# One 96-row product for the sink columns of both heads, written beside the second head's transposes

## The chip, the cores and the metric

The kernel runs on one core of a Trainium2 chip. The metric is the time of one execution on the device in microseconds (us). The core's engines are called TensorE (PE in rows; PEld is its weight load), VectorE (DVE), ScalarE (ACT), GpSimd (POOL) and SyncE (SP, which only issues transfers here).

## The reference

Attention with a sliding window and a few sink positions, then a feed-forward layer with a gate:

```python
scores = scale * q @ k^T                      # 4 batches, 8 heads, 768 positions, head size 64
keep = is_sink | ((rel >= 0) & (rel < window))   # n_sink = 4, window = 128
a = softmax(where(keep, scores, -1e9))
x = (a @ v)  -> (3072, 512)                   # heads side by side
h = x @ w_in                                  # 512 -> 2048
out = (h * clip(h + 3, 0, 6) / 6) @ w_out     # 2048 -> 512
```

## The kernel before

**Tiling.** The positions of a batch fall into three *units* of 256 queries. A unit has four *pairs* of heads (two heads of 64 rows fill 128 partitions), so there are 12 units and 48 pairs. In the first unit of a batch the sinks lie in the window's own tiles; in the other two units they don't, and the first 16 positions (SK) are handled apart. This concerns 32 of the 48 pairs, and these alone are changed. Attention of one pair is interleaved with the feed-forward layer of an earlier unit, whose products fill TensorE.

**Precision.** Most products are made of three terms, high*high, low*high and high*low: each operand is split into a rounded high part and the remainder. `high` is made by a copy (ScalarE or VectorE), `low` by a subtraction on VectorE.

**Order.** The first 14 pairs follow a list that a planner writes (`in_order`). From then on a loop over steps `s` runs eight stages (`STAGES`, L827), each a string of short names, and after each stage one piece of the feed-forward layer is issued (`drain(1)`: 12 products `hps` of 256 columns, or 6 products `o` of 512). The engines execute in just this order. In step s the pair s-1 is scored, normalised and transposed (`C`, `t0`, `t1`, `X`, `c`, `N`, `S`, `D0`, `D1`), and the pair s-2 is multiplied with the values (`E0`, `E1`) and put together (`a0`, `a1`, `b0`, `b1`, `x`). `F` runs what the feed-forward layer owes on ScalarE and VectorE (`gf`, `gh`, `g`). The pool `ps` for TensorE's results has eight banks under one tag (`bank`), handed out as they come free.

**The sinks before.** `S` (C_sinks) takes the probabilities of the 16 sink columns of both heads and both query tiles out of `Pt` and splits them into `ssc` (per tile 64 columns: high of both heads, low of both heads). `D1` (D_pt of head 1) transposes head 1's probabilities into the bank `pt`, and between these transposes TensorE turns `ssc` around by a product with the identity into a bank of its own, `spt` (64 rows x 256). At the start of the next step ScalarE copies that to `pz` (`z`, D_sinks). In `E0` and in `E1` each head then multiplies `pz` with its own 128 columns of `vs` (the sink values, high and low) as the last of the seven products that add up in `av`:

```python
seq += [low[0], (sinks["v"][:, p, vsl], d["pz"], acc)]      # L637, once per head
```

`a0`, `a1` (E_low, ScalarE) move one half of `av` to `tmp`, `b0`, `b1` (E_sum, VectorE) add the other half, and `x` (E_split, VectorE) splits `tmp` into `xh` and `xl`, the feed-forward layer's input.

Of the kernel before, what the change touches and what calls it, by code (L numbers as in the profile page):

```python
# [10 lines left out]
F32 = mybir.dt.float32  # L11
F32R = mybir.dt.float32r
# [192 lines left out]
def attn_ffn_kernel(ctx: ExitStack, tc: tile.TileContext, qx, kx, vx, vfx, vsx, n_sink, window, w_in, w_out, out):  # L205
# [87 lines left out]
    def weng(which, at):  # L293
        return {"D": nc.vector, "P": nc.gpsimd, "A": nc.scalar}[which[at % len(which)]]
# [52 lines left out]

    ssc = work.tile([P, 2, 4 * SK], F32R, name="ssc", bufs=1)
    pz = work.tile([P, UT], F32R, name="pz", bufs=1)
# [14 lines left out]
    def batch_loads(b):  # L364
        if not sinks:
            sinks["v"] = work.tile([P, NP, 4 * D], F32R, tag="vs", name="vs", bufs=1)
            nc.gpsimd.memset(sinks["v"].bitcast(F32), 0.0)
        v4 = sinks["v"][0:4 * SK].rearrange("p a (h d) -> p a h d", h=4)
        raw_s = work.tile([P, NP, 2, D], F32, tag="st", name="raw_s", bufs=3)[0:4 * SK]
        nc.sync.dma_start(out=raw_s, in_=vsx[b])  # L370
        sinks["to"] = (v4, raw_s)

    def batch_split():
        v4, raw_s = sinks["to"]
        split_parts(nc, v4[:, :, 0::2, :], v4[:, :, 1::2, :], raw_s, nc.scalar, nc.vector)

    SSE = "DD"
    START = 9
    GHI, GLO = "AD", "DD"
    XHI, XLO = "DDA", "DD"  # L380

# [160 lines left out]
    def C_sinks(s):  # L542
        u = pus[s][1]
        d = st_[s]
        if u:

            ss = ssc.rearrange("p t (k h y) -> p t k h y", k=2, h=2)
            snk_in = d["P"].rearrange("p h t w -> p h (t w)")[:, :, 2 * P:2 * WP].rearrange(
                "p h (t y) -> p t h y", t=2)[:, :, :, 0:SK]
            split_parts(nc, ss[:, :, 0], ss[:, :, 1], snk_in, weng(SSE, 0), weng(SSE, 1))  # L550

    def D_pt(s, h):
        b, u, p = pus[s]
        d = st_[s]
        blocks = ((0, P), (1, 0)) if u else ((0, 0), (1, 0), (1, P))
        pt = ps.tile([P, 512], F32, tag="bank", name="pt")
        if u and h == 1:
            d["spt"] = ps.tile([P, 512], F32, tag="bank", name="spt")
        for j, (t, c) in enumerate(blocks):
            nc.tensor.transpose(out=pt[:, j * P:(j + 1) * P], in_=cell(s, h, t, c, c + P), identity=ident)  # L560
            if u and h == 1:
                nc.tensor.matmul(out=d["spt"][0:4 * SK, t * P:(t + 1) * P], lhsT=ssc[:, t, :], rhs=ident_r,
                                 start=True, stop=True)
        d[f"pt{h}"] = pt
# [36 lines left out]
    def D_sinks(s):  # L601
        u = pus[s][1]
        d = st_[s]
        if u:
            nc.scalar.copy(out=pz[0:4 * SK], in_=d["spt"][0:4 * SK, 0:UT])
            d["pz"] = pz

    def E_av(s, h):
# [13 lines left out]
        if plain(s):  # L622
            pf = d[f"pt{h}"]
            seq = [(VS[:, slot, h, :], pf[:, c:c + o1 - o0], d["av"][:, 0, o0:o1]) for slot, c, o0, o1 in ops]
        else:

            ph, pl = d[f"pt{h}"]
            vsl = slice(2 * D * h, 2 * D * (h + 1))
            vhi = slice(2 * D * h, 2 * D * h + D)
            high = [(VS[:, slot, vsl], ph[:, c:c + o1 - o0], acc[:, o0:o1]) for slot, c, o0, o1 in ops]  # L630
            low = [(VS[:, slot, vhi], pl[:, c:c + o1 - o0], acc[0:D, o0:o1]) for slot, c, o0, o1 in ops]
            seq = [high[0]]
            for a, l in zip(high[1:], low[1:]):
                seq += [a, l]

            if u:
                seq += [low[0], (sinks["v"][:, p, vsl], d["pz"], acc)]  # L637
            else:
                seq.append((VS[:, 0, vsl], pl[:, 0:UT], acc))
        for j, (l, r, o) in enumerate(seq):  # L640
            nc.tensor.matmul(out=o, lhsT=l, rhs=r, start=(j == 0 and (h == 0 or not plain(s))),  # L641
                             stop=(j == len(seq) - 1 and (h == 1 or not plain(s))))
        if h == 1:
            E_x(s)

# [22 lines left out]
    def E_sum(s, h):  # L668
        d = st_[s]
        rows = d["tmp"][ROWS[h]]  # L670
        nc.vector.tensor_tensor(out=rows, in0=d["av"][ROWS[h], h, :], in1=rows, op=ALU.add)

    def E_split(s):
# [127 lines left out]
    def do(name, e):  # L801
# [18 lines left out]
        else:  # L820
# [5 lines left out]

    STAGES = ("b F z", "C F t0 V1", "E0 E1 t1 m F Kh Qh", "F a0 a1 X Kl Ql b0 b1", "c V2 F N", "S F x v", "D0 F vs p0 o0",  # L827
              "D1 F p1 o1 L")

    def stage(s, steps):  # L830
# [10 lines left out]
                  "b0": lambda: E_sum(e, 0), "a1": lambda: E_low(e, 1), "b1": lambda: E_sum(e, 1),  # L841
                  "x": lambda: E_split(e)}
        for step in steps.split():
# [143 lines left out]
def _layout(q, k, v, n_sink, window, moe_w_in, moe_w_out):  # L987
# [25 lines left out]
    for h in range(2):  # L1013
        vfx[:, :, :, :, h, h] = vp[:, :, 0:2 * T, h].reshape(B, NP, 2, T, D).transpose(0, 1, 3, 2, 4)
    vsx = _np.zeros((B, 4, 16, NP, 2, D), v.dtype)
    for r in range(4):
        vsx[:, r, :, :, r % 2] = vp[:, :, 0:16, r % 2].transpose(0, 2, 1, 3)
# [4 lines left out]
            'vfx': vfx.reshape(B, NP, T, 2, 2, 2 * D),  # L1022
            'vsx': vsx.reshape(B, 64, NP, 2, D), 'n_sink': n_sink, 'window': window, 'w_in': w_in, 'w_out': w_out}

# [25 lines left out]
```

## Time and profile before

| | |
|---|---|
| median of 3 runs | 712.82 us (712.49 to 713.53) |
| profiled execution, its own time | 712.8 us |
| its span, first to last instruction | 711.0 us |
| TensorE busy / weight loads busy | 700.6 us (99%) / 623.6 us (88%) |
| VectorE busy / ScalarE busy | 505.4 us (71%) / 447.7 us (63%) |
| mean granted clock of TensorE | 0.999 of full speed |

The span is what the rows below cover; 1.8 us of the execution lie outside it. Products on TensorE overlap in the records (each is entered with its whole passage through the array), so the step from one start to the next is what a product costs, not its duration.

### The profile page before, as it was taken

Reading aid. Unit: us, or ns where it says so; the run is one execution under the profiler, and the core shown is the slowest. Engines: PE = TensorE matmul, PEld = TensorE weight load, DVE = VectorE, ACT = ScalarE, POOL = GpSimd, SP = SyncE. Lnnn points to the kernel's source line nnn. Section 1 sums busy time; section 2 is a strip of 40 time slices with the busy share of each in tenths; the row PEclk is TensorE's granted clock in tenths of the full one; section 3 lists DMA queues with packets and bytes.
Section 4 is the critical chain, followed back from the end, with each engine's and each line's share of the span. In section 5 each row is a group of like instructions: output and inputs, shape, how many; then the busy total and the mean of one; then the engine's idle time right before and its main releaser. Section 6 shows DMA issues by size and latency. Waiting matters only on the chain.

```text
span 711.0 us, 13205 instructions
## 1 busy us (share of the span) xinstructions
PE 700.6 (99%) x4940; PEld 623.6 (88%) x4940; DVE 505.4 (71%) x1327; ACT 447.7 (63%) x1171; POOL 4.9 (1%) x18
## 2 busy tenths in 40 slices
PE   8999999999999999999999999999999999999996
PEld 7888988898989898889988898889898989899995
DVE  5999997445677777777777777777777877775221
ACT  5999876655675666566656566566656665754222
POOL 2000000000000000000000000000000000000000
PEclk9999999999999999999999999999999999999999
DMA  7675662120111111211111012101111111100000
GB/s 250 195 217 186 194 207 72 61 67 27 39 62 60 31 49 43 68 31 61 31 61 60 31 39 89 32 31 61 60 40 31 61 58 35 60 12 0 31 1 35
DMA packets 29481, 49.45 MB, mean 70 GB/s; under 512 B 3552, under 2 KB 20448, under 8 KB 29408
## 3 DMA queue, kind: packets, MB, share of 16 engines
q1 hardware_dynamic: 29120, 48.51, 21.3%
q8 instruction: 41, 0.67, 0.4%
q14 instruction: 32, 0.26, 0.1%
q10 hardware_dynamic: 288, 0.00, 0.0%
HBM read 42.21 MB, written 6.29 MB: 68 GB/s over the span
## 4 chain that ended last, share of the span: by engine, by line
PE 82%; ACT 7%; DVE 6%; DMA 3%; issue 1%; ACTq 0%; DVEq 0%; SPq 0%
PE o L724 34%; PE hps L692 33%; PE av L641 7%; PE sp L497 5%; PE pt L560 3%; ACT Ph L524 2%; DMA st<-in_w_out_dram 1%; DVE st L338 1%; DVE wt L341 1%; ACT wt L333 1%; ACT st L335 1%; ACT Ph L538 1%; DMA raw<-in_window_dram 1%; DVE wil L346 1%; DMA st<-in_w_in_dram 1%
## 5 line engine op out<-in xcount | busy, mean ns | idle before, releaser
L692 PE MATMUL hps<-xh,wih 128*128 128x256 f32 x768 | 221.9, 289 | 0.0
L692 PE MATMUL hps<-xl,wih 128*128 128x256 f32 x768 | 216.6, 282 | 0.0
L692 PE MATMUL hps<-xh,wil 128*128 128x256 f32 x768 | 216.2, 282 | 0.0
L724 PE MATMUL o<-woh,gh 128*128 128x512 f32 x384 | 155.7, 406 | 0.2 <-ACT gh L195 0.2
L724 PE MATMUL o<-woh,g 128*128 128x512 f32 x384 | 151.6, 395 | 0.7 <-DVE g L710 0.7
L724 PE MATMUL o<-wol,gh 128*128 128x512 f32 x384 | 151.0, 393 | 0.0
L692 PEld LDWEIGHTS hps<-xh,wih 128*128 128x128 f32 x768 | 144.7, 188 | 2.1 <-issue 0.7
L692 PEld LDWEIGHTS hps<-xl,wih 128*128 128x128 f32 x768 | 144.8, 189 | 1.2
L692 PEld LDWEIGHTS hps<-xh,wil 128*128 128x128 f32 x768 | 144.7, 188 | 0.0
L195 ACT ACTIVATE ph<-pm 128x512 fp32r<-128x512 f32 x64 | 40.5, 632 | 108.5 <-DVE pm L572 108.5
L704 DVE SCALAR_TENSOR_TENSOR gf<-gf,hps 128x512 f32<-128x512 f32 x96 | 65.7, 684 | 47.4 <-ACT gf L701 47.2
L701 ACT ACTIVATE gf<-hps,three 128x512 f32<-128x512 f32 x96 | 65.4, 681 | 51.3 <-PE hps L692 51.2
L710 DVE TENSOR_TENSOR g<-gf,gh 128x512 fp32r<-128x512 f32 x96 | 66.4, 691 | 40.0 <-ACT gh L195 37.8
L724 PEld LDWEIGHTS o<-woh,g 128*128 128x128 f32 x384 | 72.1, 188 | 18.1 <-DVE g L710 1.5
L724 PEld LDWEIGHTS o<-woh,gh 128*128 128x128 f32 x384 | 72.3, 188 | 16.6 <-issue 3.1
L724 PEld LDWEIGHTS o<-wol,gh 128*128 128x128 f32 x384 | 72.5, 189 | 11.0
L598 DVE TENSOR_TENSOR pl<-pm,ph 128x512 fp32r<-128x512 f32 x64 | 44.3, 693 | 44.7 <-ACT ph L195 44.7
L195 ACT ACTIVATE gh<-gf 128x512 fp32r<-128x512 f32 x91 | 56.9, 625 | 26.7 <-DVE gf L704 25.9
L524 ACT ACTIVATE Pt<-Pt,nb 128x144 f32<-128x144 f32 (+2 forms) x144 | 58.8, 410 | 1.2
L666 ACT COPY tmp<-av 64x256 f32<-64x256 f32 x72 | 26.5, 368 | 35.4 <-PE av L641 34.8
L507 DVE CUSTOM_DVE_ANT_0 Pt<-sp,m_t 128x272 f32<-128x272 f32 x128 | 48.5, 435 | 0.0
L538 ACT ACTIVATE Pt<-Pt,rc 128x144 f32<-128x144 f32 (+2 forms) x142 | 47.5, 408 | 0.0
(100 smaller groups left out, 966.5 us busy)
## 6 DMA issues: line engine op xcount, KB each, us to landing
st<-in_w_in_dram SPq DMA_DIRECT2D x16, 512.0 KB, 4.7
st<-in_w_out_dram SPq DMA_DIRECT2D x16, 512.0 KB, 4.4
kr<-in_kx_dram SPq DMA_DIRECT2D x32, 200.0 KB, 2.6
qr<-in_qx_dram SPq DMA_DIRECT2D x48, 128.0 KB, 2.8
out_dram<-ost SPq DMA_DIRECT2D x24, 256.0 KB, 2.2
vr<-in_vx_dram SPq DMA_DIRECT2D x32, 192.0 KB, 2.4
VF<-in_vfx_dram SPq DMA_DIRECT2D x12, 256.0 KB, 4.0
kr<-in_kx_dram SPq DMA_DIRECT2D x16, 128.0 KB, 3.4
```

The lines of the kernel that those rows point to most:

```text
L195: nc.scalar.mul(out=out, in_=src, mul=scale)
L497: nc.tensor.matmul(out=sp[g][:, 0:w], lhsT=l[gs], rhs=r[gs], start=(j == 0), stop=(j == len(terms) - 1))
L507: nc.vector.tensor_tensor_reduce(out=cell(s, g, t, 0, w), in0=sp[g][:, 0:w], in1=m[:, 0:w], scale=-SCALE, scalar=3.0e38, op0=ALU.add, op1= ...
L524: nc.scalar.activation(out=blk, in_=blk, func=AF.Exp, scale=-1.0, bias=d["nb"][:, i:i + 1], accum_out=d["sm"][:, i:i + 1])
L538: nc.scalar.mul(out=blk, in_=blk, mul=c)
L598: nc.vector.tensor_tensor(out=pl[:, 0:w], in0=pt[:, 0:w], in1=ph[:, 0:w].bitcast(F32), op=ALU.subtract)
L641: nc.tensor.matmul(out=o, lhsT=l, rhs=r, start=(j == 0 and (h == 0 or not plain(s))), stop=(j == len(seq) - 1 and (h == 1 or not plain(s))))
L692: nc.tensor.matmul(out=hp[:, half, :], lhsT=l, rhs=r, start=(j == 0), stop=(j == n - 1))
L701: nc.scalar.activation(out=gf, in_=hp, func=AF.Relu, bias=three, scale=1.0)
L704: nc.vector.scalar_tensor_tensor(out=gf, in0=gf, scalar=6.0, in1=hp, op0=ALU.min, op1=ALU.mult)
L710: nc.vector.tensor_tensor(out=g, in0=gf, in1=gh.bitcast(F32), op=ALU.subtract)
L724: nc.tensor.matmul(out=acc, lhsT=l[:, f, ts_], rhs=r[i][:, f, :], start=(i == 0 and f == 0 and j == 0), stop=(i == NFP - 1 and f == 1 and ...
```

## The change

The sinks leave the two heads' sums. `ssc` gets 96 columns per tile: high of both heads, the same high again, low of both heads; ScalarE makes the second copy of the high part. `vs` gets 128 columns per head pair in place of 256: its rows are ordered so that one product over 96 rows gives high*high, high*low and low*high of both heads at once, head 0 in rows 0 to 63 of the result and head 1 in rows 64 to 127. TensorE turns `ssc` around into the right half of `pt`'s bank of head 1, and the new product's result is written into that bank's left half, which the transposes used. A new step `k` (E_sinks) on VectorE adds it to `tmp`. In the loop, `x` now stands before `F` and `S` after it, and the split of the sink values (`vs`, once per batch) stands after `p0 o0`. The six products left in each head's sum stand in another order. The transfer of the sink values has 96 rows of 2 KB in place of 64, four times in all. (`XHI` loses an entry that steps from 9 on don't read.)

```diff
-    ssc = work.tile([P, 2, 4 * SK], F32R, name="ssc", bufs=1)
+    ssc = work.tile([P, 2, 6 * SK], F32R, name="ssc", bufs=1)
...
     def batch_split():
-        v4, raw_s = sinks["to"]
-        split_parts(nc, v4[:, :, 0::2, :], v4[:, :, 1::2, :], raw_s, nc.scalar, nc.vector)
+        v, raw_s, low = sinks["v"], sinks["to"], slice(2 * SK, 4 * SK)
+        copy_r(nc, nc.scalar, v[0:6 * SK], raw_s[0:6 * SK])
+        nc.vector.tensor_tensor(out=v[low], in0=raw_s[low], in1=v[low].bitcast(F32), op=ALU.subtract)
...
-            split_parts(nc, ss[:, :, 0], ss[:, :, 1], snk_in, weng(SSE, 0), weng(SSE, 1))
+            split_parts(nc, ss[:, :, 0], ss[:, :, 2], snk_in, weng(SSE, 0), weng(SSE, 1))
+            copy_r(nc, nc.scalar, ssc[:, :, 2 * SK:4 * SK], ssc[:, :, 0:2 * SK].bitcast(F32))
...
-        if u and h == 1:
-            d["spt"] = ps.tile([P, 512], F32, tag="bank", name="spt")
         for j, (t, c) in enumerate(blocks):
+            if u and h == 1:
+                nc.tensor.matmul(out=pt[0:6 * SK, UT + t * P:UT + (t + 1) * P], lhsT=ssc[:, t, :], rhs=ident_r,
+                                 start=True, stop=True)
             nc.tensor.transpose(out=pt[:, j * P:(j + 1) * P], in_=cell(s, h, t, c, c + P), identity=ident)
-            if u and h == 1:
-                nc.tensor.matmul(out=d["spt"][0:4 * SK, t * P:(t + 1) * P], lhsT=ssc[:, t, :], rhs=ident_r,
-                                 start=True, stop=True)
+        d["spt"] = pt
...
-            nc.scalar.copy(out=pz[0:4 * SK], in_=d["spt"][0:4 * SK, 0:UT])
-            d["pz"] = pz
+            nc.scalar.copy(out=pz[0:6 * SK], in_=d["spt"][0:6 * SK, UT:2 * UT])
...
-                seq += [low[0], (sinks["v"][:, p, vsl], d["pz"], acc)]
+                seq = [*high[:2], low[1], low[2], low[0], high[2]]
...
         if h == 1:
+            if u:
+                nc.tensor.matmul(out=d["spt"][:, 0:UT], lhsT=sinks["v"][:, p, :], rhs=pz, start=True, stop=True)
             E_x(s)
...
+    def E_sinks(s):
+        if pus[s][1]:
+            tmp = st_[s]["tmp"]
+            nc.vector.tensor_tensor(out=tmp, in0=st_[s]["spt"][:, 0:UT], in1=tmp, op=ALU.add)
...
-    STAGES = ("b F z", "C F t0 V1", "E0 E1 t1 m F Kh Qh", "F a0 a1 X Kl Ql b0 b1", "c V2 F N", "S F x v", "D0 F vs p0 o0",
+    STAGES = ("b F z", "C F t0 V1", "E0 E1 t1 m F Kh Qh", "F a0 a1 X Kl Ql b0 b1", "c V2 F k N", "x F S v", "D0 F p0 o0 vs",
               "D1 F p1 o1 L")
```

Three places in the order of the instructions show it. The first is TensorE at `D1`: the transposes of head 1 (`pt<-ident_r,Pt`) and the turning of the sinks (from `ssc`), ahead of the next 12 products of the feed-forward layer. A bracket names the engines whose results the instruction waits for. Before:

```order
L692 MATMUL hps<-xh_6274,wil_121 128x256
L560 MATMUL pt<-ident_r,Pt 128x128 [waits Activation_49]
L562 MATMUL spt<-ident_r,ssc 64x128 [waits DVE_49]
L560 MATMUL pt<-ident_r,Pt 128x128 [waits Activation_49]
L562 MATMUL spt<-ident_r,ssc 64x128
L692 MATMUL hps<-xh_5708,wih_113 128x256
```

In the changed kernel, at the same place:

```order
L698 MATMUL hps<-xh_6273,wil_121 128x256
L560 MATMUL pt<-ident_r,ssc 96x128 [waits DVE_49,Activation_49]
L562 MATMUL pt<-ident_r,Pt 128x128
L560 MATMUL pt<-ident_r,ssc 96x128
L562 MATMUL pt<-ident_r,Pt 128x128
L698 MATMUL hps<-xh_5707,wih_113 128x256
```

The sinks' products now stand first, write 96 rows in place of 64, and wait for VectorE and ScalarE; a transpose stands last.

The second place is TensorE at `E1`, the second head's sum, up to the first product of the feed-forward layer behind it (`ph` and `pl` are the high and low parts of the transposed probabilities, `VS` the values; 64 rows mean a product with the high values alone). Before:

```order
L641 MATMUL av<-ph,VS 128x256
L641 MATMUL av<-ph,VS 128x128
L641 MATMUL av<-pl,VS 64x128 [waits DVE_49]
L641 MATMUL av<-ph,VS 128x128
L641 MATMUL av<-pl,VS 64x128
L641 MATMUL av<-pl,VS 64x256
L641 MATMUL av<-pz,vs 128x256
L692 MATMUL hps<-xh_5708,wih_114 128x256 [waits DVE_49]
```

In the changed kernel:

```order
L640 MATMUL av<-ph,VS 128x256 [waits Activation_49]
L640 MATMUL av<-ph,VS 128x128
L640 MATMUL av<-pl,VS 64x128 x2
L640 MATMUL av<-pl,VS 64x256
L640 MATMUL av<-ph,VS 128x128
L644 MATMUL pt<-pz,vs 128x256 [waits Activation_49]
L698 MATMUL hps<-xh_5707,wih_112 128x256 [waits DVE_49]
```

The product with `pz` now writes `pt`, once for both heads; the first head's sum has the same six products as here and none with `pz`. The three 64-row products stand together, and the second `ph` product of 128 columns has moved behind them.

The third place is VectorE between the feed-forward layer's gate (`gf`) and the first masking of transposed probabilities (`pm`, step `p0`). Before:

```order
L704 SCALAR_TENSOR_TENSOR gf<-gf,hps 128x512 [waits Activation_49]
L201 CAST ssc<-Pt 128x2x32 [waits Activation_49]
L190 TENSOR_TENSOR ssc<-Pt,ssc 128x2x32 [waits DVE_49]
L710 TENSOR_TENSOR g<-gf,gh 128x512 [waits Activation_49]
L201 CAST xh_3824<-tmp 128x256
L678 TENSOR_TENSOR xl_3825<-tmp,xh_3824 128x256 [waits DVE_49]
L572 TENSOR_TENSOR pm<-pt,side 128x512 [waits PE_49]
```

In the changed kernel:

```order
L710 SCALAR_TENSOR_TENSOR gf<-gf,hps 128x512 [waits Activation_49]
L677 TENSOR_TENSOR tmp<-pt,tmp 128x256
L201 CAST xh_3823<-tmp 128x256 [waits DVE_49]
L684 TENSOR_TENSOR xl_3824<-tmp,xh_3823 128x256 [waits DVE_49]
L716 TENSOR_TENSOR g<-gf,gh 128x512 [waits Activation_49]
L201 CAST ssc<-Pt 128x2x32
L190 TENSOR_TENSOR ssc<-Pt,ssc 128x2x32 [waits DVE_49]
L572 TENSOR_TENSOR pm<-pt,side 128x512 [waits PE_49]
```

The addition of the sinks (`tmp<-pt,tmp`) and the split of `tmp` have moved ahead of `g`, and the split of the sink columns (`ssc`) behind it.

## Rows read from the trace of the kernel before

**Rows 1.** The page: the span, and each engine's busy time.

```profile
span 711.0 us, 13205 instructions
...
PE 700.6 (99%) x4940; PEld 623.6 (88%) x4940; DVE 505.4 (71%) x1327; ACT 447.7 (63%) x1171; POOL 4.9 (1%) x18
```

**Rows 2.** Chain that ended last, 480 to 520 us: start, duration, engine, line, count.

```profile
493.33 1.29 PE av L641 x14
...
501.99 0.06 PE spt L562
...
507.61 1.29 PE av L641 x14
```

**Rows 3.** Timeline of TensorE, 507.2 to 508.9 us: start, duration, instruction.

```profile
507.45 0.34 PE L641 MATMUL av<-ph,VS 128*128 128x256 f32 x2
507.62 0.22 PE L641 MATMUL av<-pl,VS 128*64 128x128 f32 x1
507.69 0.27 PE L641 MATMUL av<-ph,VS 128*128 128x128 f32 x1
507.80 0.35 PE L641 MATMUL av<-pl,VS 128*64 128x128 f32 x2
507.98 0.28 PE L641 MATMUL av<-pz,vs 128*128 128x256 f32 x1
508.10 0.34 PE L641 MATMUL av<-ph,VS 128*128 128x256 f32 x2
```

**Rows 4.** Groups of instructions, 207.4 to 650.5 us: count, busy, mean ns, idle before.

```profile
L641 PEld LDWEIGHTS av<-ph,VS 128*128 128x128 f32 x189 | 32.7, 189 | 2.7
...
L671 DVE TENSOR_TENSOR tmp<-av,tmp 64x256 f32<-64x256 f32 x62 | 25.9, 418 | 0.4
...
L497 PEld LDWEIGHTS sp<-kt,qt 64*128 64x128 f32 x360 | 24.0, 184 | 10.7 <-issue 10.7
...
L666 ACT COPY tmp<-av 64x256 f32<-64x256 f32 x62 | 22.8, 368 | 29.4 <-PE av L641 29.0
...
L641 PEld LDWEIGHTS av<-pl,VS 128*64 128x64 f32 x190 | 21.0, 135 | 0.0
...
L201 DVE CAST ssc<-Pt 128x64 fp32r<-128x64 f32 x31 | 6.1, 195 | 15.8 <-ACT Pt L538 15.8
```

**Rows 5.** Timeline of TensorE at D1, 501.3 to 502.5 us.

```profile
501.72 0.27 PE L560 MATMUL pt<-ident_r,Pt 128*128 128x128 f32 x1
...
502.06 0.33 PE L692 MATMUL hps<-xh,wih 128*128 128x256 f32 x1
502.22 0.29 PE L692 MATMUL hps<-xl,wih 128*128 128x256 f32 x1
```

**Rows 6.** Timeline of TensorE at D0, 499.5 to 500.6 us.

```profile
500.08 0.38 PE L560 MATMUL pt<-ident_r,Pt 128*128 128x128 f32 x2
...
500.42 0.28 PE L692 MATMUL hps<-xl,wih 128*128 128x256 f32 x1
```

**Rows 7.** Timeline of VectorE, 498.2 to 501.4 us; idle before and releaser in brackets.

```profile
498.28 0.69 DVE L704 SCALAR_TENSOR_TENSOR gf<-gf,hps 128x512 f32<-128x512 f32 x1 [0.29 <-ACT gf L701]
499.50 0.20 DVE L201 CAST ssc<-Pt 128x64 fp32r<-128x64 f32 x1 [0.53 <-ACT Pt L538]
...
500.03 0.69 DVE L710 TENSOR_TENSOR g<-gf,gh 128x512 fp32r<-128x512 f32 x1
500.64 0.29 DVE L201 CAST xh<-tmp 128x256 fp32r<-128x256 f32 x1
...
501.30 0.68 DVE L572 TENSOR_TENSOR pm<-pt,side 128x512 f32<-128x512 f32 x1
```

**Rows 8.** Timeline of ScalarE, 499.3 to 502.1 us.

```profile
499.37 0.62 ACT L195 ACTIVATE gh<-gf 128x512 fp32r<-128x512 f32 x1
502.02 0.63 ACT L195 ACTIVATE ph<-pm 128x512 fp32r<-128x512 f32 x1 [2.02 <-DVE pm L572]
```

**Rows 9.** Timeline of VectorE at the first mask of the next scores, 507 us.

```profile
507.63 0.08 DVE L507 DVE_READ_ACCUMULATOR2_ANT nb<- 128x1 f32 x1
```

More of the change, by code (lines that the diff above doesn't have):

```diff
@@ L365, in batch_loads @@
         if not sinks:
-            sinks["v"] = work.tile([P, NP, 4 * D], F32R, tag="vs", name="vs", bufs=1)
+            sinks["v"] = work.tile([P, NP, 2 * D], F32R, tag="vs", name="vs", bufs=1)
             nc.gpsimd.memset(sinks["v"].bitcast(F32), 0.0)
[L368 to L371, printed above, removed]
+        raw_s = work.tile([P, NP, 2 * D], F32, tag="st", name="raw_s", bufs=3)
+        nc.sync.dma_start(out=raw_s[0:6 * SK], in_=vsx[b])
+        sinks["to"] = raw_s
     def batch_split():
-        v4, raw_s = sinks["to"]
-        split_parts(nc, v4[:, :, 0::2, :], v4[:, :, 1::2, :], raw_s, nc.scalar, nc.vector)
+        v, raw_s, low = sinks["v"], sinks["to"], slice(2 * SK, 4 * SK)
+        copy_r(nc, nc.scalar, v[0:6 * SK], raw_s[0:6 * SK])
+        nc.vector.tensor_tensor(out=v[low], in0=raw_s[low], in1=v[low].bitcast(F32), op=ALU.subtract)
     SSE = "DD"
@@ L379, in attn_ffn_kernel @@
     GHI, GLO = "AD", "DD"
-    XHI, XLO = "DDA", "DD"
+    XHI, XLO = "DA", "DD"
     def eng(which, s):
@@ L545, in C_sinks @@
         if u:
-            ss = ssc.rearrange("p t (k h y) -> p t k h y", k=2, h=2)
+            ss = ssc.rearrange("p t (k h y) -> p t k h y", k=3, h=2)
             snk_in = d["P"].rearrange("p h t w -> p h (t w)")[:, :, 2 * P:2 * WP].rearrange(
                 "p h (t y) -> p t h y", t=2)[:, :, :, 0:SK]
-            split_parts(nc, ss[:, :, 0], ss[:, :, 1], snk_in, weng(SSE, 0), weng(SSE, 1))
+            split_parts(nc, ss[:, :, 0], ss[:, :, 2], snk_in, weng(SSE, 0), weng(SSE, 1))
+            copy_r(nc, nc.scalar, ssc[:, :, 2 * SK:4 * SK], ssc[:, :, 0:2 * SK].bitcast(F32))
     def D_pt(s, h):
@@ L841, in stage @@
                   "b0": lambda: E_sum(e, 0), "a1": lambda: E_low(e, 1), "b1": lambda: E_sum(e, 1),
-                  "x": lambda: E_split(e)}
+                  "k": lambda: E_sinks(e), "x": lambda: E_split(e)}
         for step in steps.split():
@@ L1014, in _layout @@
         vfx[:, :, :, :, h, h] = vp[:, :, 0:2 * T, h].reshape(B, NP, 2, T, D).transpose(0, 1, 3, 2, 4)
-    vsx = _np.zeros((B, 4, 16, NP, 2, D), v.dtype)
-    for r in range(4):
+    vsx = _np.zeros((B, 6, 16, NP, 2, D), v.dtype)
+    for r in range(6):
         vsx[:, r, :, :, r % 2] = vp[:, :, 0:16, r % 2].transpose(0, 2, 1, 3)
@@ L1022, in _layout @@
             'vfx': vfx.reshape(B, NP, T, 2, 2, 2 * D),
-            'vsx': vsx.reshape(B, 64, NP, 2, D), 'n_sink': n_sink, 'window': window, 'w_in': w_in, 'w_out': w_out}
+            'vsx': vsx.reshape(B, 96, NP, 2 * D), 'n_sink': n_sink, 'window': window, 'w_in': w_in, 'w_out': w_out}
 def kernel(**inputs):
```

## The prediction, made before the changed kernel ran

> **What bounds the kernel now.** I read the page first. TensorE is busy 99% of the span [rows 1], but its records overlap, so that share alone decides nothing; weight loads stand at 88%, VectorE at 71%, ScalarE at 63%. Next, the chain of waits, which says whether the others ever hold TensorE up. In the stretch that has the changed pairs it runs through TensorE alone: from one pair's value products at 493.33 us to the next pair's at 507.61 [rows 2] it names no other engine, and the step is 14.28 us. Idle time in the groups agrees: ScalarE waits for TensorE before moving `av` to `tmp`, 29.0 us in 62 instructions, most of it before the first of each pair, so nearly 1 us a pair [rows 4]. So in this stretch TensorE sets the pace, and every tenth of a microsecond taken from its 32 changed pairs is 3.2 us of the end, as long as no new wait reaches it. Each piece below is costed by the step from start to start on TensorE.
>
> **The value products.** In the first head's sum, two products of 256 and 128 columns take 507.45 to 507.62 (0.17), a 64-row product of 128 columns 0.07, one of the same 128 columns with all 128 rows 0.11, two 64-row products of 128 and 256 columns 0.18, and the sinks' product 0.12, up to 508.10: together 0.65 [rows 3]. The second head's run on to 508.74 by the same pattern, and the chain gives 1.29 for both [rows 2]. One step is odd: 0.11 for a product that streams no more columns than the 0.07 one ahead of it. Its weights have 128 columns and their load takes 189 ns, against 135 ns for 64 columns [rows 4]; the 54 ns between them is about what the step is too long, and the product it has to load behind is the shortest there is. I read that as a weight load not covered.
>
> The change takes out two products of 0.12 and puts one of 0.12 back. The other six per head keep their columns: 0.17, then 64-row products of 0.06 and 0.18, then the full-width one of 128 columns, now loaded behind 256 columns and so 0.06 long; but what follows it (the other head's first product, or the sinks' product) has 128 columns of weights to load behind that short one, which I charge the same 0.05. That is 0.52 a head, 1.04 for two, with the sinks' product 1.16. Against 1.29 the gain is 0.13 a pair. Bounds: 0.23, if what follows the short product loads without a stall; 0.03, if both places stall.
>
> **Turning the sinks (D1).** From the first transpose at 501.72 to the second product behind it at 502.22 are 0.50; less the 0.12 of one product, 0.38 [rows 5]. A transpose costs 0.11: at D0, two of them and one product take 0.34 [rows 6]. A turning product costs 0.06 [rows 2]. Two of each are 0.34, so some 0.04 to 0.05 are lost behind the last turning product, again a 128-column load behind a short product. With a transpose last, as at D0, nothing is lost behind it. The weights of the turning product grow from 64 columns to 96; they load behind a 256-column product and behind a transpose, both of them longer than the 54 ns that even 64 more columns cost. I take 0.05 gained a pair; bounds 0.05 gained and, if the larger loads stick out by half of 54 ns each and the end gains nothing, 0.05 lost.
>
> The Trainium skill (TensorE: Matmul & The Clock Gate, LDWEIGHTS) has a load grow with its columns, at 1.2 columns per ns; that would be 53 ns for 64 columns, and the 54 ns above agree. From it I estimate 27 ns more for the 96-column load.
>
> **What VectorE and ScalarE get.** VectorE gains the addition of 128x256 per pair. The nearest row, the addition of 64x256 out of the same memory, takes 0.42 [rows 4]. Its place is the hole after the gate: the gate ends at 498.97 and VectorE idles 0.53 waiting for ScalarE's normalised probabilities [rows 7], 15.8 us over 31 pairs [rows 4]. The new order fills that hole with work that has been ready for long: addition from 498.95 to 499.38, the split of `tmp` (0.66 from `xh` to `pm`), `g` at 500.05, when `gh` is there (ended 499.99, [rows 8]), then the two `ssc` instructions (`g` holds 0.61, the pair 0.53), `pm` at 501.2 against 501.30 before [rows 7]. So nothing behind it gets later, and I charge nothing; without the hole it would be 0.42 later, which still has to use up ScalarE's wait for TensorE first.
>
> ScalarE gains the third copy of the sink columns. It waits for VectorE's first `ssc` instruction, by the above finished at 500.86, and behind it in ScalarE's order stands the first head's `ph`, which waits for `pm` anyway and before which ScalarE idles 2.02 [rows 8]. The copy's cost isn't in the trace: below it lies VectorE's 0.20 for the same shape [rows 4], above it ScalarE's 0.62 for eight times the elements [rows 8]; 64 elements a row are nearer the lower end, I take 0.3. It lands at 501.2, by the upper bound at 501.5.
>
> Two waits of TensorE are new. The first turning product waits for that copy. TensorE would load its weights some 0.11 ahead of 501.72, at 501.61, since nothing between the last value product and D1 gets shorter: a margin of 0.4, at the upper bound 0.1. Behind it would stand the transposes, 12 products, and on VectorE `pm` of head 1. And `pt` of head 1 now stays taken up to the addition, while the bank of `spt` falls away: the value sum takes the bank that the gate has read, the next `hps` that of the first score mask, whose last record ends at 507.71 [rows 9]. TensorE comes for that weight load at 508.49 (508.74 less 0.12 for the load's lead and 0.13 gained): margin 0.78. The split of the sink values is as long as before in columns (512) and four times only; moving it behind `p0` delays the masks by at most one such instruction, 0.7 (a row of that width, [rows 7]), still inside the 0.78. The wider transfer is 64 KB four times.
>
> **Sum.** 32 pairs times (0.13 + 0.05) are 5.8 us. The profiled execution took 712.8 us, 711.0 in the span and 1.8 outside; it equals the median, 712.82. Forecast 707.0 us. A measurement of this kernel can tell about 0.2% from no change, 1.4 us.
>
> **Rivals.**
>
> *Slower: D1 waits for the third copy.* The order puts three engines in a row (probabilities, VectorE's split, ScalarE's copy, TensorE) where two were. For it: the margin is a tenth at the upper bound. Against: the copy would have to land at 501.61 + 0.18 = 501.79 to use up the gain, and 0.23 past 501.61 to make it slower by 1.4 us; that is 0.6 later than I lay it out. Were VectorE's row 0.5 later and the copy 0.62 long, D1 would stall 0.4 a pair: 707.0 + 12.8 = 719.8. Chance 6%.
>
> *No change: the next `hps` waits for the mask.* It takes back what the products give if the mask comes 0.78 + 0.18 = 0.96 later. ScalarE and VectorE follow TensorE with waits of their own, so I see no source of that much. 712.8, chance 5%.
>
> *Weight loads set the pace.* Then a product's streamed columns don't count, only weight columns: one load of 128 fewer (0.107, twice the 54 ns) and twice 32 more (0.054), a gain of 0.053 a pair: 711.1 us. For it: 88% busy. Against: transposes and 256-column products cover their successors' loads in rows 5 and 6. Chance 6%. The Trainium skill (Trainium Kernel Development and Optimization, Performance Expectations) names the weight loads' busy share, with the use made of the peak, as the good measure of how near TensorE is to its limit, rather than the products' busy share; by that alone this rival would come out.
>
> *Each change between 64 and 128 rows of output costs TensorE a drain.* Before the scores, whose products use 64 rows of input, TensorE's loads idle 10.7 us over 31 pairs, 0.35 each [rows 4], so a drain exists there. If the 0.05 losses were such drains, one per change of width, the change would remove eight of them a pair (four of eight in the sums, four of four at D1), 0.40, besides the product's net 0.12: 32 x 0.52 = 16.6 us, 696.2. Against: the step from a 64-row product of 256 columns to the sinks' product with 128 rows is 0.12, as long as without a change [rows 3]. Chance 3%. The Trainium skill (TensorEngine Tiling (Array Packing), Key Properties) states that changing the tiling mode drains TensorE; for 64-column tiles these rows don't agree.
>
> **Numbers.** The forecast has 80%; its own range is 705.0 (0.06 of the 0.10 charged behind the short products doesn't show: 2 us) to 709.4 (D1 loses 0.025 in place of gaining 0.05). At the lower bound of one of the two terms (0.03 and 0.05, or 0.13 and a loss of 0.05) it is 0.08 a pair, 710.2, the upper end of the range. Outside lie all four rivals, 20% together. Faster by over 0.2% (below 711.4): forecast, drains and most of the loads case, 88%; within 0.2%: 6%; slower: 6%.
>
> **What the changed profile would show.** Value products of a pair with the sinks' product some 1.16 us in the chain, D1 0.34 from its first turning product to the first product behind the last transpose; a step from pair to pair of 14.1; no idle time of weight loads before `pt` or before the `hps` behind the sinks' product; VectorE's wait for ScalarE before `ssc` gone. It would be wrong if the step were 14.28 again, with a wait of TensorE for ScalarE at D1 or for VectorE at `hps` in the table of waits.

## The result, and the profile after

The changed kernel took 707.35 us (median of 4 executions, 705.34 to 707.82), the kernel before, on the same chip, 713.17 (4 executions, 712.49 to 714.18). The ratio is 0.9912, with a 95% interval of 0.9888 to 0.9936: the change made the kernel faster, by about 0.9%. The forecast was 707.0 us.

The page of the changed kernel; its first lines answer to [rows 1].

```profile
span 705.1 us, 13207 instructions
...
PE 695.7 (99%) x4908; PEld 618.5 (88%) x4908; DVE 514.7 (73%) x1359; ACT 455.8 (65%) x1203; POOL 4.5 (1%) x18
```

The shares of TensorE and of its weight loads are the same 99% and 88% as before, though the kernel became faster: these shares don't tell the two kernels apart. VectorE did 9.3 us more work and ScalarE 8.1 more, and the span doesn't show it. TensorE has 32 instructions fewer: two products of each changed pair went, one came.

The chain of waits, 480 to 520 us, answers to [rows 2].

```profile
490.03 1.00 PE av L640 x12
491.03 0.17 PE pt L644
491.20 2.85 PE hps L698 x24
494.05 2.79 PE o L730 x12
...
498.49 0.06 PE pt L560
498.55 0.11 PE pt L562
498.66 0.06 PE pt L560
498.72 0.11 PE pt L562
498.83 1.43 PE hps L698 x12
...
504.18 1.00 PE av L640 x12
```

The chain still runs through TensorE alone. From pair to pair it is 504.18 - 490.03 = 14.15 us, where it was 14.28. The value products with the sinks' product (`pt L644`) take 1.17 in place of 1.29. D1 is 0.06 + 0.11 + 0.06 + 0.11 = 0.34, and so were the same four pieces in the other order. In the chain the gain of D1 shows behind it: its 12 `hps` take 1.43, where the kernel before has

```profile
502.22 1.49 PE hps L692 x12
```

The timeline, which enters each product at its start, divides it otherwise. D1 of the changed kernel, 498.1 to 499.2 us, answers to [rows 5]:

```profile
498.32 0.22 PE L560 MATMUL pt<-ident_r,ssc 128*96 128x128 f32 x1
...
498.59 0.36 PE L698 MATMUL hps<-xh,wih 128*128 128x256 f32 x1
498.79 0.27 PE L698 MATMUL hps<-xl,wih 128*128 128x256 f32 x1
```

From D1's first start to that of the next `hps` are 0.27 here and 0.34 before (501.72 to 502.06). On average over the pairs it is 0.263 in place of 0.340, of which the 12 `hps` behind give back 0.030, so that 0.046 a pair are left.

One pair may lie some hundredths off, so here and below "the step" is a mean: thirty steps inside the loop, from the start of one pair's first value product to that of the next. In the kernel before they run from 206.92 to 636.29 us, 14.31 each; in the changed one from 207.07 to 631.27, 14.14. The difference is 0.172, over thirty steps 5.17 us, and at 32 changed pairs 5.5. The spans differ by 5.9, but 0.8 of that lies behind the start of TensorE's last product (703.94 us before, 698.88 after), where results are only moved out; that last stretch is 6.2 to 7.2 us in the fourteen profiles of this study, and no run explains its differences.

The timeline of TensorE, 504.0 to 505.3 us: start, duration, instruction. It answers to [rows 3].

```profile
504.02 0.34 PE L640 MATMUL av<-ph,VS 128*128 128x256 f32 x2
...
504.96 0.22 PE L640 MATMUL av<-ph,VS 128*128 128x128 f32 x1
505.02 0.34 PE L644 MATMUL pt<-pz,vs 128*128 128x256 f32 x1
505.19 0.28 PE L698 MATMUL hps<-xh,wih 128*128 128x256 f32 x1
```

The last short product starts at 504.96, the sinks' product at 505.02, and the next `hps` at 505.19: 0.17 for a product of 256 columns that takes 0.12 in the sums of before. Its record is 0.34 long, where that of an `hps` product of the same shape is 0.28: the wait for its 128-column load behind the short product lies inside it. From 504.02 to 505.19 are 1.17; 1.16 were forecast, with one such stall in each head.

The timeline of VectorE, 494.5 to 498.6 us, idle time and its releaser in brackets, answers to [rows 7].

```profile
494.88 0.69 DVE L710 SCALAR_TENSOR_TENSOR gf<-gf,hps 128x512 f32<-128x512 f32 x1 [0.47 <-ACT gf L707]
495.48 0.42 DVE L677 TENSOR_TENSOR tmp<-pt,tmp 128x256 f32<-128x256 f32 x1
495.93 0.29 DVE L201 CAST xh<-tmp 128x256 fp32r<-128x256 f32 x1
...
497.23 0.19 DVE L201 CAST ssc<-Pt 128x64 fp32r<-128x64 f32 x1
...
497.59 0.68 DVE L572 TENSOR_TENSOR pm<-pt,side 128x512 f32<-128x512 f32 x1
```

No idle time is left between the gate and `pm`; the addition (L677) and the split stand where 0.53 of waiting was. `pm` starts 2.02 behind the gate's end (495.57), where it started 2.33 behind it before (498.97 to 501.30).

Groups of instructions over the whole span, which answer to [rows 4]: output, input, count, busy time, mean ns of one, idle time before.

```profile
L667 ACT COPY tmp<-av 64x256 f32<-64x256 f32 x72 | 26.5, 368 | 33.0 <-PE av L640 32.5
L677 DVE TENSOR_TENSOR tmp<-pt,tmp 128x256 f32<-128x256 f32 x32 | 13.3, 417 | 0.0
...
L560 PEld LDWEIGHTS pt<-ident_r,ssc 128*96 128x96 f32 x64 | 10.5, 164 | 0.0
L195 ACT ACTIVATE ssc<-ssc 128x64 fp32r<-128x64 f32 x32 | 8.2, 258 | 28.5 <-DVE ssc L201 28.5
...
L201 DVE CAST ssc<-Pt 128x64 fp32r<-128x64 f32 x32 | 6.0, 188 | 0.0
```

The addition takes 0.417 us, as the 64-row one did, the third copy of the sinks 0.258, and the 96-column load 164 ns. VectorE no longer idles before `ssc` (0.0, was 15.8), TensorE's loads don't idle before the turning product (0.0), and ScalarE still waits for TensorE before moving `av`. The 28.5 us that ScalarE idles before the third copy cost nothing, since its next work, `ph`, waits for `pm` behind it anyway.

### The profile page after: what moved, and what is told of

Same layout as the page of the kernel before. It is cut to its first block, busy times and chain, and to the rows that moved or that the text cites. A ratio compares the mean times of both kernels' runs of the same rounds, so it can differ in the third digit from the quotient of the medians.

```text
span 705.1 us, 13207 instructions
## 1 busy us (share of the span) xinstructions
PE 695.7 (99%) x4908; PEld 618.5 (88%) x4908; DVE 514.7 (73%) x1359; ACT 455.8 (65%) x1203; POOL 4.5 (1%) x18
## 4 chain that ended last, share of the span: by engine, by line
PE 82%; ACT 6%; DVE 6%; DMA 4%; issue 1%; ACTq 0%; DVEq 0%; SPq 0%
PE o L730 34%; PE hps L698 33%; PE av L640 6%; PE sp L497 5%; PE pt L562 3%; DMA st<-in_w_in_dram 2%; ACT Ph L524 2%; DMA st<-in_w_out_dram 1%; DVE st L338 1%; DVE wt L341 1%; ACT wt L333 1%; ACT st L335 1%; ACT Ph L538 1%; PE pt L644 1%; DMA raw<-in_window_dram 1%
```

## The experiments

The theory: TensorE sets the pace, and the gain is (a) one product of 0.12 less a pair and (b) at D1, weight loads that no longer stick out behind a short product; the new work of the other engines lies in holes. Rivals: drains at changes between 64 and 128 output rows, a pace set by the loads' own columns, waits that the move of the stages removes, and, on the slow side, the wait of D1 for the third copy. All twelve in one table; ratios are to the kernel before on the same chip.

| kernel | median us | ratio, 95% interval | step |
|---|---|---|---|
| before | 713.17 | 1 | 14.31 |
| changed | 707.35 | 0.9912 [0.9888, 0.9936] | 14.14 |
| 1 turning product last | 708.64 | 0.9937 [0.9921, 0.9954] | 14.20 |
| 2 short products in a row | 713.59 | 1.0015 [1.0005, 1.0025] | 14.34 |
| 3 before, turning product first | 711.90 | 0.9982 [0.9972, 0.9992] | 14.27 |
| 4 before, stages moved | 713.23 | 1.0001 [0.9991, 1.001] | 14.33 |
| 5 no addition | 706.55 | 0.9909 [0.9893, 0.9926] | 14.14 |
| 6 sinks' product twice | 710.86 | 0.9971 [0.9959, 0.9984] | 14.26 |
| 7 third copy made twice | 707.16 | 0.993 [0.9914, 0.9945] | 14.14 |
| 8 third copy made four times | 717.77 | 1.0068 [1.0051, 1.0085] | 14.49 |
| 9 turning product of 128 columns | 709.03 | 0.9943 [0.9925, 0.9961] | 14.18 |
| 10 turning product of 112 columns | 707.22 | 0.9928 [0.9913, 0.9944] | 14.17 |
| 11 sums ahead of the scores | 709.02 | 0.9947 [0.9934, 0.9961] | 14.18 |
| 12 as 11, sink values split last | 708.46 | 0.9946 [0.9932, 0.9959] | 14.15 |

### 1. The changed kernel with the turning product last again

```diff
+            nc.tensor.transpose(out=pt[:, j * P:(j + 1) * P], in_=cell(s, h, t, c, c + P), identity=ident)
             if u and h == 1:
...
-            nc.tensor.transpose(out=pt[:, j * P:(j + 1) * P], in_=cell(s, h, t, c, c + P), identity=ident)
```

> The changed kernel with the old order at D1: a transpose first, the turning product (96 columns) behind it, twice. Theory of the uncovered loads: the product behind the last turning product must load 128 columns behind a short one again, 0.05 to 0.06 a pair lost: step from pair to pair 14.19 to 14.20 (14.14 in the changed kernel), 1.6 to 1.9 us more, about 709.1. Drain theory: a 96-column product is entered with 128 rows of the array like its neighbours, no change of width either way, so nothing: 14.14 and 707.4.

The chain of waits at its D1:

```profile
500.14 0.11 PE pt L559
500.25 0.06 PE pt L561
500.31 1.48 PE hps L698 x12
```

The pieces (the first two, alike, stand ahead of these) are those of the changed kernel in the other order, and what stands behind them grew: 12 products take 1.48 in place of 1.43. The step is 0.056 longer by the order alone, with the same products and loads: a 128-column load stands behind the 0.06 product again. Of the 0.056, D1 and the 12 `hps` behind it hold 0.044; the rest is spread over the other pieces.

### 2. The changed kernel with the short products in a row

```diff
-                seq = [*high[:2], low[1], low[2], low[0], high[2]]
+                seq = [high[0], *low, high[1], high[2]]
```

> The changed kernel with each head's six value products in another order: the 256-column one with 128 rows, the three 64-row ones (short, short, long put as 256, 128, 128 columns), then the two short ones with 128 rows. As many changes of width per head as in the changed kernel (two), but three 128-column loads stand behind short products in place of one. Theory of the uncovered loads: 2 x 0.05 a head, 0.2 a pair, step 14.34, 707.4 + 6.4 = 713.8. Drain theory: 0, 14.14 and 707.4.

The chain of waits:

```profile
493.49 1.20 PE av L640 x12
494.69 0.17 PE pt L644
```

The same products take 1.20 in place of 1.00, 0.05 for each of four places where a 128-column load now follows a short product and didn't before. It has as many changes between 64 and 128 output rows as the changed kernel, two in each head's six products, and is 0.20 a pair slower: with drains at those changes it had to take the same. The whole gain of the change is gone, 1.0015 of the time before; so a bad order of the six products that stayed costs more than the product saved. The changed order gains nothing by itself, though: a head had one such place before (the 0.11 in [rows 3]) and has one now (behind its last short product), so the 0.115 gained in the sums is the product that went.

### 3. The kernel before with the turning product first

```diff
-            nc.tensor.transpose(out=pt[:, j * P:(j + 1) * P], in_=cell(s, h, t, c, c + P), identity=ident)
             if u and h == 1:
                 nc.tensor.matmul(out=d["spt"][0:4 * SK, t * P:(t + 1) * P], lhsT=ssc[:, t, :], rhs=ident_r,
                                  start=True, stop=True)
+            nc.tensor.transpose(out=pt[:, j * P:(j + 1) * P], in_=cell(s, h, t, c, c + P), identity=ident)
```

> The kernel before with one part of the change alone: at D1 the turning product (64 columns, in its own bank) stands ahead of the transpose. Theory of the uncovered loads: 0.05 to 0.06 a pair gained, step 14.25 on average in place of 14.31, 1.6 to 1.9 us, about 711.4. Drain theory: 128, 64, 128, 64, 128 rows is as many changes as before: nothing, 14.31 and 713.2.

The step is 0.04 shorter, and 0.0018 of the time is 1.3 us, a little less than the 1.6 expected. At D1 and in the 12 `hps` behind it 0.047 are gained: the turn alone, without any other part of the change, gives its term there.

### 4. The kernel before with the stages of the changed one

```diff
-    STAGES = ("b F z", "C F t0 V1", "E0 E1 t1 m F Kh Qh", "F a0 a1 X Kl Ql b0 b1", "c V2 F N", "S F x v", "D0 F vs p0 o0",
+    STAGES = ("b F z", "C F t0 V1", "E0 E1 t1 m F Kh Qh", "F a0 a1 X Kl Ql b0 b1", "c V2 F N", "x F S v", "D0 F p0 o0 vs",
```

> The kernel before with the moves of the stages alone: the split of the value sum ahead of the feed-forward layer's part, the split of the sink columns behind it, the split of the sink values behind the first head's transposes. Theory that TensorE's own products are the gain: ordinary steps stay 14.28 to 14.32, and only the eight steps at the ends of units, 14.35, lose the 0.05 for which a product waits there for the split: at most 0.5 us, 712.7 to 713.2. Rival, that the order of VectorE's work brought much of the gain: steps near 14.14, 707 to 710.

No gain: 1.0001, step 14.33. The long steps at the ends of units fell from 14.35 to 14.33, but the others rose to it from 14.28 to 14.32, against what was expected of them. Moving `x` ahead and the sink values' split back gives nothing by itself; in the kernel before VectorE's wait behind the gate cost TensorE nothing.

### 5. The changed kernel without the addition

```diff
-        if pus[s][1]:
+        if False:
```

> The changed kernel without VectorE's addition of the sinks to the pair's sum (the output lacks the sinks' share). Theory that the addition lies in VectorE's former hole: the same step, 14.14, and 707.4 within 0.2%; the masking of head 0's transposes comes up to 0.36 earlier. Rival, that VectorE's new work costs time at the end: 0.1 a pair or more faster, 704 or less.

The step is 14.14, the same to a thousandth (424.20 us over thirty in both), and the time within the spread of the changed kernel's. The addition's 0.417 us is hidden in full.

### 6. The sinks' product twice

```diff
-                nc.tensor.matmul(out=d["spt"][:, 0:UT], lhsT=sinks["v"][:, p, :], rhs=pz, start=True, stop=True)
+                for _ in range(2):
+                    nc.tensor.matmul(out=d["spt"][:, 0:UT], lhsT=sinks["v"][:, p, :], rhs=pz, start=True, stop=True)
```

> The changed kernel with the sinks' product issued twice into the same place (the second writes the same numbers again). Theory that TensorE's streamed columns set the pace: one product more of 256 columns, its load covered by the first: 0.12 a pair, step 14.26, 707.4 + 3.8 = 711.2. Theory that what was gained came from the engines behind TensorE (an earlier split, fewer waits): nothing, 14.14. Theory that weight columns alone set the pace: 0.107 a pair, 710.8.

The chain of waits has it in one line:

```profile
492.86 0.29 PE pt L645 x2
```

0.29 for two against 0.17 for one, and the step grew by 0.117: a product of 256 columns costs 0.12, also when its weights are those of the product ahead. Those weights are loaded again, in 190 ns like the first, so this kernel by itself tells little between the 0.12 and the 0.107 of the expectation.

### 7 and 8. The third copy made twice, and four times

The edit of kernel 7; kernel 8 has `range(4)`. In both, the host also fills fewer of the six row groups of the sink values (`vsx`), two in kernel 7 and four in kernel 8, and leaves the others zero; what the device executes is the same but for the copies.

```diff
-            copy_r(nc, nc.scalar, ssc[:, :, 2 * SK:4 * SK], ssc[:, :, 0:2 * SK].bitcast(F32))
+            for _ in range(2):
+                copy_r(nc, nc.scalar, ssc[:, :, 2 * SK:4 * SK], ssc[:, :, 0:2 * SK].bitcast(F32))
```

> The changed kernel with ScalarE's third copy of the sink columns made twice. It ends 0.29 later, still 0.2 ahead of the first turning product's load, by the margin of 0.5 read in the changed kernel: nothing, step 14.14, 707.4, no row of TensorE's loads waiting for the copy. Three more copies made TensorE wait 9.3 us in 32 times; if that wait grew from the first copy on, rather than from a margin, one more would cost 0.1 a pair, 14.24 and 710.5.

> The changed kernel with ScalarE's third copy of the sink columns made four times in a row (each waits for the one before it, some 0.29). In the changed kernel the copy ended 0.5 us ahead of the load of the first turning product. Three more end 0.87 later, so TensorE should wait 0.35 to 0.45 a pair at D1: step 14.5 to 14.6, 707.4 + 11 to 14 = 718 to 722, with a row in the table of waits. Rival, that other work of TensorE takes the wait up or the margin is larger than read: 14.14 and 707.4.

Twice costs nothing: step 14.14. Four times, the table of waits (engine, what waited <- for what: us, times, longest) has a line that the changed kernel lacks:

```profile
PEld pt L561 <- ACT ssc L195: 9.3, 32, 0.4
```

TensorE's load waits for the copy in each of the 32 pairs, the step grows by 0.35, and the time is above that of the kernel before. So the slower rival's mechanism exists; it needs the copy some half a microsecond later. The timeline of ScalarE has the four copies as one row:

```profile
503.98 1.12 ACT L195 ACTIVATE ssc<-ssc 128x64 fp32r<-128x64 f32 x4 [0.86 <-DVE ssc L201]
```

Three more copies, each behind the end of the one before it, are 1.12 - 0.26 = 0.86, of which 0.35 showed: the margin was about 0.5. The changed kernel's timelines of ScalarE and of the loads say the same, since the copy ends at 497.71 and the first turning load starts at 498.21:

```profile
497.45 0.26 ACT L195 ACTIVATE ssc<-ssc 128x64 fp32r<-128x64 f32 x1 [0.86 <-DVE ssc L201]
498.21 0.16 PEld L560 LDWEIGHTS pt<-ident_r,ssc 128*96 128x96 f32 x1
```

### 9 and 10. The turning product with 128 and with 112 columns

The edit of kernel 9; kernel 10 has `7 * SK` in both places. The columns added hold zeros.

```diff
-    ssc = work.tile([P, 2, 6 * SK], F32R, name="ssc", bufs=1)
+    ssc = work.tile([P, 2, 8 * SK], F32R, name="ssc", bufs=1)
...
-                nc.tensor.matmul(out=pt[0:6 * SK, UT + t * P:UT + (t + 1) * P], lhsT=ssc[:, t, :], rhs=ident_r,
+                nc.tensor.matmul(out=pt[:, UT + t * P:UT + (t + 1) * P], lhsT=ssc[:, t, :], rhs=ident_r,
```

> The changed kernel with turning products of 128 columns in place of 96 (the last 32 are zeros). Theory of the uncovered loads: a load of 128 columns (0.107) is covered by the 256-column product and by the transpose (0.11) ahead of it: nothing, 14.14 and 707.4. Theory that weight columns set the pace: twice 27 ns a pair, 14.19, 709.1.

> The changed kernel with turning products of 112 columns (the last 16 are zeros). 128 columns cost 0.038 a pair although both loads stand behind products that cover such a load elsewhere. If a turning product's load has a fixed length that sticks out beyond the 0.113 of the product ahead (133 ns read for 128 columns, 13 ns less per 16 columns): 0.005 to 0.015 a pair, step 14.15, 707.4 to 707.8. If weight columns as such set the pace: 0.027 a pair, 14.167, 708.2. If 128 is a step of its own (the full width): nothing, 14.14.

The chain of waits at D1 of the kernel with 128 columns:

```profile
499.51 0.06 PE pt L561
499.57 0.13 PE pt L563
499.70 1.43 PE hps L699 x12
```

And of the one with 112, with the products of the feed-forward layer ahead of it:

```profile
490.95 2.88 PE hps L699 x24
493.82 2.75 PE o L731 x12
...
498.47 0.12 PE pt L563
```

With 128 columns the step grew by 0.038, between the numbers of the two theories. The turning products start as before; the pieces of the transposes behind them are 0.13 in place of 0.11. Averaged over the pairs, D1's four products, from the first start to that of the `hps` behind, take 0.266 with 64 columns (kernel 3), 0.263 with 96 (the changed kernel), 0.277 with 112 and 0.302 with 128. Nothing is lost up to 96 columns; from 112 to 128 each of the two turning products costs 0.013 more. A load of 128 columns takes 198 ns, one of 112 takes 182: 16 ns more. So the load does stick out, but only from a size between 96 and 112 columns on, and both theories in kernel 9's expectation were too coarse: a pace set by load columns would have shown from 64 to 96, and full cover would have held to 128. The time of the kernel with 112 columns can't be told from that of the changed one, and of its step, 0.027 longer, only 0.013 is at D1, within the 0.005 to 0.015 that its first theory had. The rest lies elsewhere: all 48 `hps` of a step take 0.056 more (24 of them 2.88 in place of 2.85), and the 24 `o` take 0.041 less (12 of them 2.75 in place of 2.79). So the step as a whole, which came out at the 14.167 of the second theory, doesn't speak for that theory.

### 11 and 12. The sums ahead of the scores

Of the two stalls a pair that are left, one stands behind the second head's last short product. In kernel 11 the sinks' product stands ahead of that short product, and the scores, whose load has 64 rows, behind it.

```diff
-    STAGES = ("b F z", "C F t0 V1", "E0 E1 t1 m F Kh Qh", "F a0 a1 X Kl Ql b0 b1", "c V2 F k N", "x F S v", "D0 F p0 o0 vs",
+    STAGES = ("b F z", "E0 E1 C F t0 V1", "t1 m F Kh Qh", "F a0 a1 X Kl Ql b0 b1", "c V2 F k N", "x F S v", "D0 F p0 o0 vs",
...
         for j, (l, r, o) in enumerate(seq):
+            if h == 1 and u and j == len(seq) - 1:
+                nc.tensor.matmul(out=d["spt"][:, 0:UT], lhsT=sinks["v"][:, p, :], rhs=pz, start=True, stop=True)
...
-            if u:
-                nc.tensor.matmul(out=d["spt"][:, 0:UT], lhsT=sinks["v"][:, p, :], rhs=pz, start=True, stop=True)
```

> The changed kernel with the value sums moved ahead of the next pair's scores, and the sinks' product ahead of the second head's last short product. By the theory of the uncovered loads one of the two left in the sums goes: the sinks' product then loads behind 256 columns, and behind the short product stand the scores, which wait there for the array to empty anyway. 0.05 a pair: step 14.09, 1.6 us less, 705.8. Against it the second head's low part is needed 1.2 us earlier: in three or four pairs that also split a batch's sink values it may be late by 0.2 to 0.4, so 705.8 to 707.2. Rival, that the scores' wait grows by as much: 14.14.

It missed. The chain of waits in the middle of a batch:

```profile
503.41 0.94 PE av L642 x11
504.36 0.12 PE pt L641
504.48 0.06 PE av L642
504.54 0.95 PE sp L497 x12
...
507.07 2.88 PE hps L698 x24
```

The products of the sums take 1.12 in place of 1.17, so the stall did go. But 24 `hps` take 2.88 in place of 2.85 and the other pieces a few thousandths each, and the step there is 14.12 to 14.15, as in the changed kernel. Besides, at each start of a batch one step is 14.48. The timeline of TensorE there:

```profile
206.43 0.46 PE L642 MATMUL av<-pl,VS 128*64 128x128 f32 x3 [0.18 <-DVE pl L598]
```

VectorE splits the sink values once a batch, 0.68 us, ahead of the second head's low part `pl`, and the sums, which now come earlier, wait for it. Kernel 12 moves that split behind `pl`:

```diff
-    STAGES = ("b F z", "E0 E1 C F t0 V1", "t1 m F Kh Qh", "F a0 a1 X Kl Ql b0 b1", "c V2 F k N", "x F S v", "D0 F p0 o0 vs",
-              "D1 F p1 o1 L")
+    STAGES = ("b F z", "E0 E1 C F t0 V1", "t1 m F Kh Qh", "F a0 a1 X Kl Ql b0 b1", "c V2 F k N", "x F S v", "D0 F p0 o0",
+              "D1 F p1 o1 vs L")
```

> As the run before it (sums ahead of the scores), with the split of the sink values moved from behind the first head's parts to the end of the step, so that VectorE does it after the second head's low part. There, at each start of a batch, VectorE's split (203.58, 0.68) stood ahead of that low part, the first head's second short product waited for it (206.43), and the step was 14.48 in place of 14.14, five times. Theory, the split was the cause: the five long steps go back to 14.14, the time falls by 5 x 0.34 = 1.7, 709.0 to 707.3 us (706.7 to 707.7), about that of the changed kernel. Rival, something else at a batch's start holds the low part (the masks, the bank): the steps stay at 14.48 and the time at 709.0. The steps inside a batch should stay at 14.13 in either case, since the 0.05 saved at the last short product came back there as longer products of the feed-forward layer.

The long steps fell to 14.28, not to 14.14. The timeline of TensorE at the same place shows where the rest is:

```profile
206.20 0.36 PE L641 MATMUL pt<-pz,vs 128*128 128x256 f32 x1
206.39 0.22 PE L642 MATMUL av<-ph,VS 128*128 128x128 f32 x1
```

And that of VectorE:

```profile
205.37 0.68 DVE L375 TENSOR_TENSOR vs<-raw_s,vs 32x512 fp32r<-32x512 f32 x1
```

No wait for `pl` is left, but the sinks' product, which needs the split itself, takes 0.27 in the chain there in place of 0.12: VectorE ends the split at 206.05, too late by 0.15. The split was the cause; it had only been moved to the next one who waits for it. The fifth long step, the loop's first (14.45 in both, 13.81 in the changed kernel), didn't move, against what was expected, and it has another cause. It belongs to a pair without sinks apart, and the table of waits of that stretch (kernel 12, 150 to 163 us) has a line that the changed kernel's lacks:

```profile
PEld pt L562 <- ACT Pt L538: 0.8, 2, 0.5
```

TensorE's transposes wait for the probabilities (`Pt`) that ScalarE normalises, and ScalarE comes to them late: its part of the gate starts at 152.75, where the changed kernel has 152.01. That the sums, which now stand ahead of the 12 `hps` that the gate waits for, make it late is likely; no run shows it. No kernel of this study that does the whole computation beats the changed one by more than the spread of its runs.

## Why the prediction was right, point by point

**TensorE's chain is the end.** Right: 0.172 less a step is 5.5 us in 32 pairs, where the forecast had 0.18 and 5.8. That the medians differ by 5.8 as well is in part luck. The two terms of the sum measured 0.115 + 0.046 = 0.161 a pair, 5.2 us. Another 0.015 a step was gained in the 12 `hps` ahead of D1, for which the prediction had no term; kernel 3 shows none of it, kernel 4 a half, and its cause is open. In the profiles TensorE's last product starts 5.1 us earlier, and 0.8 us lie in the stretch behind it, which the prediction didn't treat. The prediction gives its upper end twice, as 709.4 and as 710.2; 707.35 is below both.

**The value products, 0.13.** Measured 0.115, averaged over the pairs (1.290 to 1.175, with the sinks' product), so the term was a little too large. Its parts hold: a product out and in is 0.12 (kernel 6), and behind the short product 0.05 shows, once a head (kernels 2 and 11). The reading of one odd step of 0.11 as a load that isn't covered held: with four such places more, kernel 2 lost 0.20. This term needed it only to know that nothing changes there, one such place a head before and after; the term for D1 hangs on it.

**Turning first, 0.05.** Measured 0.046 (0.340 to 0.263 at D1, of which the 12 `hps` behind give back 0.030); in the same two places 0.044 by kernel 1 and 0.047 by kernel 3. The 0.34 that the prediction named as a sign was no test, since in the chain D1 was 0.34 before as well. What the prediction gave as the reason for the larger load being free, that what it loads behind is longer than 54 ns, was too generous: 96 columns are free and 112 are not quite. The change lies just inside.

The load itself grew from 138 to 164 ns for 32 columns more, 26 ns. The Trainium skill (TensorE: Matmul & The Clock Gate, LDWEIGHTS), from whose rate I had estimated 27, agrees.

**The addition, hidden.** Right: 0.42 taken, 0.417 measured, nothing on the path (kernel 5). `pm` came 0.3 earlier after the gate, not 0.1: the 0.53 charged to the two `ssc` instructions was read from a place where `g` behind them still waited for `gh` (to 499.99, [rows 8]), and in the changed kernel they take 0.36 (497.23 to 497.59).

**The third copy, 0.3, landing 0.4 ahead of its use.** Measured 0.258, and 0.5 ahead, by the timeline and by kernel 8.

**The `hps` behind the sinks' product waits for no mask.** Right: no wait of TensorE for VectorE stands in the chain there.

**The rivals.** The wait for the copy: a real mechanism with margin (kernels 7 and 8). The mask: not seen. Loads set the pace: falls, since kernels 1 and 2 load the same columns as the changed kernel and are 0.056 and 0.20 a step slower, and since going from 64 to 96 columns at D1 costs nothing (0.266 to 0.263). The loads' busy share, 88% before and after, didn't rank the two kernels. The Trainium skill (Trainium Kernel Development and Optimization, Performance Expectations) names it, with the use made of the peak, as a good metric of how close a kernel is to its roofline; here the share gave no help in telling the faster kernel. Drains as the source of the 0.05 losses: fall by kernel 2. The Trainium skill (TensorEngine Tiling (Array Packing), Key Properties) states that a change of tiling mode drains TensorE; for tiles of 64 and 128 columns in these sums no run here shows it.

## What to carry to other kernels

Where one engine's chain is the whole step, price an edit by the steps from start to start on it, and look for a step longer than its columns. In the value sums here a load of 128 columns showed by 0.05 behind a product of 128 streamed columns, also when longer ones stood ahead of that (kernel 2), and not behind one of 256; a load of 64 columns was hidden behind either. So a long load belongs behind a long product and a short load behind a short one. A bad order of the products that stay can cost more than the product that goes. Before giving a hidden engine new work, find its hole and measure the margin by doing the work several times; and before moving a stage forward, see what is done once a batch ahead of its input.

## What was not expected of the hardware

The cover of the turning load ends between 96 and 112 columns, though the first of the two stands behind a product of 256 columns, where the `hps` products hide loads of 128. What grows is the piece of the transpose behind the turning product. The transpose's own load does come late: on average it starts 0.133 and 0.154 (first and second) behind the start of the turning load with 128 columns, where it is 0.119 and 0.111 with 96. Why it can't start earlier, no run took apart.

The same products took different times in kernels that differ elsewhere: 24 `hps` 2.85 in the changed kernel's loop, 2.88 in kernels 10, 11 and 12; 12 `o` 2.79 and, in kernel 10, 2.75, also behind the last changed pair. There, in the changed kernel itself, 24 `hps` take 2.84 and 2.88 in turn. In kernel 10 a tile is larger, so that what is placed behind it in memory may move; but in kernel 9 the same tile is larger still, and the products take 2.85 and 2.79 as in the changed one. The cause is open.
